# The order of the first six attention units in an attention and experts kernel on one Trainium2 core

## The chip, the core and the metric

The kernel runs on one core of a Trainium2 chip. It uses TensorE (PE: matmuls, with weight loads shown apart as PEld), VectorE (DVE), ScalarE (ACT), GpSimd (POOL) and the DMA queues that SyncE (SP), ACT and POOL fill. The metric is the device time of one execution in microseconds; lower is better. A profile is one execution, taken by the hardware profiler.

## The reference

Block-sparse attention (4 batches, 8 heads, 768 tokens, head size 64, blocks of 32), then a mixture of 4 experts in which every token uses every expert.

```python
mask = np.abs(blk_i - blk_j) <= 1                      # own block and its two neighbours
mask |= (blk_i == 0) | (blk_j == 0) | (blk_i == n_blocks - 1) | (blk_j == n_blocks - 1)
for qb in range(n_blocks):
    for kb in sampled_blocks[qb]:                      # three sampled blocks for each block
        mask[qb * 32:(qb + 1) * 32, kb * 32:(kb + 1) * 32] = True
scores = np.where(mask, q @ k.T / 8, -1e9)
attn = softmax(scores) ; x = attn @ v                  # x: 3072 tokens x 512
for e in range(4):
    h = np.maximum(x @ w1[e], 0.0)                     # 512 -> 1024
    out += p[:, e:e+1] * (h @ w2[e])                   # 1024 -> 512
```

## The kernel before, in words

An inner block of 32 queries sees eight blocks of keys: three neighbours, the two end blocks and three sampled ones. Four such blocks make a group `t` of 128 queries, and a group is done in two **units** (`u` = 0 and 1, four heads each). Before the experts can start, three groups of batch 0 must be done: units 0 to 5, groups 0 to 2. This document calls that stretch the **opening**. After it the expert products keep PE busy, with the other attention units put between them.

A unit n (class `Group`) goes through these steps. `S(n)`: scores on PE (L304 against the neighbours in `k`, L309 against the gathered keys `kr`), 64 matmuls, then on DVE four maxima with the mask (L319) and on ACT four exponentials (L322). `T(n)`: eight transposes of the probabilities on PE (L331) in two halves, the first copied to `pt` by ACT and the second by DVE (L333). `A(n)`: 64 matmuls with the values (L359), then on DVE the reciprocal sums `rec` (L348, L349) and the weighting into `xg` (L377). `X(n)`, for odd n: four transposes of the group's result (L403), then `tokens` casts it to the experts' operand `xo` on ACT (L281) and puts the rest on DVE (L282).

What the units need: keys `kr` of a group are copied inside SBUF by POOL, ACT and DVE (L149 end blocks, L156 sampled blocks, whose number is read into a register first, L141). Values `v` of a group are two tiles: neighbours by SP (L175) and sampled rows by four gathers that POOL issues (L179, `DMA_INDIRECT`); the end blocks' values lie in `ends` and are copied in (`put_ends`, L852). There are four value tiles, so group 2 reuses those of group 0 when `A(1)` has read them. The mask is made from index tables on POOL and DVE and spread to rows by one matmul (L256).

The experts' weights come as `w1` (`load_w1`, L580, 512 KB; two halves s = 0, 1 for each of eight chunks c) and `w2` (`load_w2`, L585, 256 KB). A half of `w1` becomes four operands `wo`: ACT casts (L597), POOL makes the rest (L598). A `w2` tile becomes `h` (ACT, L635) and `l` (POOL, L636) in `split_w2`. Seven `wo` are made before the first product; each product then asks for the next. A `w1` load must wait until POOL is done with the fourth `wo` of the half that lies in its buffer, a `w2` load until POOL has made `l` of the tile in its buffer. A first-layer product pair (L662, two `wo`) writes the accumulators `v` and `w` in turn; ACT takes the result by a ReLU (`hh`, L671) and DVE the rest (`hl`, L672), and only then is the accumulator free again. Second-layer matmuls are L732.

All five engines run their instructions in the order in which the program writes them; SP issues its loads in that order too, and one that must wait holds those behind it.

Of the kernel before, what the change touches and what calls it, by code (L numbers as in the profile page):

```python
# [17 lines left out]
P = 128  # L18
BLOCK = 32
# [4 lines left out]
def attention_moe_kernel(ctx: ExitStack, tc, qb, kb, vr, sampled, sampled_t, probs, w1, w2, out):  # L24
# [37 lines left out]
    pool["k"] = setup.enter_context(tc.tile_pool(name="k1", bufs=8))  # L62
# [73 lines left out]
    def copier(j, r):  # L136
        return nc.scalar if j <= QG and r == 2 else COPIERS[r % len(COPIERS)]

    def sampled_block(j, r):
        if (j, r) not in regs:  # L140
            regs[j, r] = copier(j, r).value_load(sbrow[:1, j * NR + r, :1], min_val=0, max_val=NB - 1)  # L141
        return regs[j, r]
# [15 lines left out]

    def end_rows(b):
        return bass.AP(vr.tensor, vr[b * S:b * S + BLOCK].offset,  # L160
                       [[DM, BLOCK], [(NB - 1) * BLOCK * DM, 2], [1, DM]])
# [7 lines left out]
    def load_v(b, t, cs=range(QG)):  # L169
        js = blocks(t)  # L170
        for c in range(min(cs), min(max(cs) + 1, len(js)), 2):
# [3 lines left out]
            nc.sync.dma_start(v[:3 * BLOCK, :n, 0],  # L175
                              bass.AP(rows.tensor, rows.offset,
                                      [[DM, 3 * BLOCK], [BLOCK * DM, n], [1, DM]]))
            for i in range(n):
# [11 lines left out]
    for c in range(QG):  # L190
        for r in (1, 2):
            sampled_block(1 + c, r)
# [28 lines left out]
                   allow_small_or_imprecise_dtypes=True)  # L221
    bad = p1.tile([NB, SLOTS], F32, name="bad")
    sbf = p1.tile([NB, NR], F32, name="sbf")
    d = p1.tile([NB, NR], F32, name="d")
    nc.gpsimd.memset(bad, 0.0)
    nc.vector.tensor_copy(sbf, sbi[:, :, 0])
# [7 lines left out]
    for r in range(1, NR):  # L234
        for e in range(r):
# [3 lines left out]
    ind = p1.tile([NB, NG, P], F32, name="ind")  # L239
    nc.gpsimd.memset(ind, 1.0)  # L240
    nc.gpsimd.affine_select(out=ind, in_=ind, pattern=[[P, NG], [1, P]], compare_op=ALU.is_ge,
                            fill=0.0, base=BLOCK, channel_multiplier=-BLOCK)
    nc.gpsimd.affine_select(out=ind, in_=ind, pattern=[[-P, NG], [-1, P]], compare_op=ALU.is_ge,
                            fill=0.0, base=-1, channel_multiplier=BLOCK)
    ind4 = p1.tile([NB, P], F32, name="ind4")
    nc.vector.reduce_sum(ind4, ind.rearrange("n t p -> n p t"), axis=AX.X)
    sel = p1.tile([NB, NG, SLOTS], F32, name="sel")
    nc.gpsimd.memset(sel, -BIG)
    nc.gpsimd.affine_select(out=sel, in_=sel, pattern=[[-QG, NG], [0, SLOTS]], compare_op=ALU.is_ge,
# [781 lines left out]
```

## Time and profile before

| | us |
|---|---|
| time, median of 3 runs (lowest to highest) | 1254.86 (1254.47 to 1259.41) |
| the profiled execution: its own time | 1257.47 |
| the profiled execution: span of its instructions | 1255.6 |
| first expert product starts (in the span) | 49.17 |
| PE busy in the span | 1231.8 (98%) |

Times in rows count from the start of the span. In a row of a timeline stand the start, the length, the engine, the line, the operation, what it writes and reads with sizes, how many instructions were merged, and in brackets how long the engine stood idle before and what ended that. "issue" means that the engine waited for nothing that the profile shows.

### The profile page before, as it was taken

How to read it: one execution, taken by the hardware profiler on the slowest of the kernel's cores; microseconds unless marked ns; L12 is line 12 of the kernel's file. 1: busy time of each engine (PE TensorE's matmuls, PEld its weight loads, DVE VectorE, ACT ScalarE, POOL GpSimd, SP SyncE). 2: the span in 40 equal slices, each digit the busy share in tenths (PEclk: the TensorE clock that was granted, in tenths of full speed). 3: DMA queues.
4: the chain of work that ended last, by engine and by line, in shares of the span. 5: the costliest groups of instructions: out<-in, count | busy, mean ns of one | idle time of the engine just before them, and what ended most of it. 6: DMA issues, size and time to landing. Idle time of an engine off the chain costs nothing.

```text
span 1255.6 us, 31597 instructions
## 1 busy us (share of the span) xinstructions
PE 1231.8 (98%) x12242; PEld 1072.5 (85%) x12242; DVE 753.9 (60%) x1735; ACT 679.5 (54%) x1826; POOL 719.0 (57%) x848
## 2 busy tenths in 40 slices
PE   6899999999999999999999999999999999999998
PEld 4788888888888888888888888888888899999997
DVE  6455535555458675666658676665756855555553
ACT  5556645666655546666555455666664544444441
POOL 6566556666659545555547655556544855555550
PEclk9899999999999999999999999999999999999999
DMA  9546555655535325332323433333321222222211
GB/s 258 181 128 170 153 183 170 192 174 173 159 111 188 110 68 156 98 118 90 111 86 120 145 102 100 103 119 114 118 77 43 93 93 67 68 68 68 67 51 51
DMA packets 64113, 149.02 MB, mean 119 GB/s; under 512 B 7707, under 2 KB 9244, under 8 KB 63964
## 3 DMA queue, kind: packets, MB, share of 16 engines
q1 hardware_dynamic: 58294, 129.70, 32.9%
q0 software_dynamic: 5632, 17.31, 5.1%
q8 instruction: 96, 1.57, 0.5%
q14 instruction: 53, 0.43, 0.1%
q10 hardware_dynamic: 38, 0.00, 0.0%
HBM read 140.69 MB, written 6.29 MB: 117 GB/s over the span
## 4 chain that ended last, share of the span: by engine, by line
PE 67%; DVE 1%; issue 1%; POOL 0%; POOLq 0%; DVEq 0%
PE po L732 33%; PE w L683 16%; PE v L683 12%; PE o L359 2%; PE tp L331 1%; PE s L309 1%; PE s L304 1%; DVE oacc L747 1%; PE ow L469 1%; PE sw L418 1%; PE tw L440 0%; DVE r L619 0%; POOL wo L612 0%; DVE r L617 0%; PE v L662 0%
## 5 line engine op out<-in xcount | busy, mean ns | idle before, releaser
L612 POOL TENSOR_TENSOR wo<-r,wo 128x256 fp32r<-128x256 f32 x288 | 241.1, 840 | 279.7 <-ACT wo L611 278.1
L732 PE MATMUL po<-h,hh 128*128 128x512 f32 x768 | 310.2, 404 | 1.3 <-DVE oacc L747 1.1
L732 PE MATMUL po<-h,hl 128*128 128x512 f32 x768 | 302.6, 394 | 0.0
L732 PE MATMUL po<-l,hh 128*128 128x512 f32 x768 | 301.7, 393 | 0.0
L683 PE MATMUL w<-xo,wo 128*128 128x384 f32 x1152 | 236.1, 340 | 0.0
L636 POOL TENSOR_TENSOR l<-r,h 128x512 fp32r<-128x512 f32 x160 | 211.4, 1321 | 37.5 <-ACT h L635 37.0
L683 PEld LDWEIGHTS w<-xo,wo 128*128 128x128 f32 x1152 | 207.5, 188 | 18.0 <-DVE z L718 0.7
L683 PE MATMUL v<-xo,wo 128*128 128x384 f32 x864 | 175.9, 338 | 0.0
L732 PEld LDWEIGHTS po<-h,hl 128*128 128x128 f32 x768 | 144.2, 188 | 33.0
L683 PEld LDWEIGHTS v<-xo,wo 128*128 128x128 f32 x864 | 154.4, 188 | 12.3 <-ACT z L710 0.2
L732 PEld LDWEIGHTS po<-h,hh 128*128 128x128 f32 x768 | 144.2, 188 | 19.6 <-DVE oacc L747 2.9
L598 POOL TENSOR_TENSOR wo<-r,wo 128x256 fp32r<-128x256 f32 x128 | 95.3, 747 | 114.7 <-ACT wo L597 109.3
L732 PEld LDWEIGHTS po<-l,hh 128*128 128x128 f32 x768 | 145.2, 189 | 11.4
L611 ACT CAST wo<-r 128x256 fp32r<-128x256 f32 x288 | 114.5, 398 | 49.7 <-PE w L683 32.2
L747 DVE SCALAR_TENSOR_TENSOR oacc<-po,pr,oacc 128x512 f32<-128x512 f32 x168 | 124.3, 742 | 24.6 <-PE po L732 24.4
L322 ACT ACTIVATE p<-p,mx 128x256 f32<-128x256 f32 (+1 forms) x192 | 95.5, 499 | 69.4 <-DVE mx L319 67.5
L635 ACT CAST h<-r 128x512 fp32r<-128x512 f32 x160 | 99.3, 620 | 11.8 <-PE po L732 11.8
L179 POOL DMA_INDIRECT v<-in_vr_dram,vidx x88 | 85.7, 974 | 26.3 <-issue 16.6
L319 DVE CUSTOM_DVE_ANT_1 p<-s,mask 128x256 f32<-128x256 f32 (+1 forms) x192 | 69.9, 418 | 46.3 <-PE s L309 45.9
L662 PE MATMUL v<-xo,wo 128*128 128x384 f32 x384 | 79.9, 345 | 0.5 <-ACT xo L281 0.5
L706 DVE TENSOR_TENSOR p<-w,p 128x384 f32<-128x384 f32 x48 | 26.7, 556 | 89.4 <-PE w L683 82.3
L662 PE MATMUL w<-xo,wo 128*128 128x384 f32 x384 | 79.1, 341 | 0.0
(139 smaller groups left out, 1723.4 us busy)
## 6 DMA issues: line engine op xcount, KB each, us to landing
r<-in_w_dram SPq DMA_DIRECT2D x80, 512.0 KB, 4.0
r<-in_w_dram SPq DMA_DIRECT2D x160, 256.0 KB, 2.7
v<-in_vr_dram SPq DMA_DIRECT2D x44, 384.0 KB, 4.8
k<-in_kb_dram SPq DMA_DIRECT2D x8, 768.0 KB, 5.7
v<-in_vr_dram SPq DMA_DIRECT2D x12, 512.0 KB, 5.1
out_dram<-oacc SPq DMA_DIRECT2D x23, 256.0 KB, 2.5
q<-in_qb_dram SPq DMA_DIRECT2D x20, 256.0 KB, 5.2
v<-in_vr_dram SPq DMA_DIRECT2D x24, 128.0 KB, 3.4
```

The source lines that it names most:

```text
L179: nc.gpsimd.indirect_dma_start(out=v[:G, i, 1], out_offset=None, in_=vr, element_offset=b * S * DM, in_offset=bass.IndirectOffsetOnAxis(ap ...
L319: nc.vector.tensor_tensor_reduce(p.rearrange("p (a b) -> p a b", b=BLOCK), s[h][:n, i], mk, -SCALE, 3.0e38, ALU.add, ALU.min, mx[:n])
L322: nc.scalar.activation(p, p, AF.Exp, bias=mx[:n], scale=-1.0, accum_out=self.sums[:n, m:m + 1])
L598: nc.gpsimd.tensor_sub(o[:, 1], r[s][:, i, k], f32(o[:, 0]))
L611: nc.scalar.copy(o[:, 0], src)
L612: nc.gpsimd.tensor_sub(o[:, 1], src, f32(o[:, 0]))
L635: nc.scalar.copy(h, r)
L636: nc.gpsimd.tensor_sub(l, r, f32(h))
L662: nc.tensor.matmul(W[s], w[:, wi, t], x[xi][:, k * KH + t], start=k == 0 and m == 0, stop=k == 1 and m == 3 * KH - 1)
L683: nc.tensor.matmul(ps, w[:, wi, t], x[:, xi, t], start=fresh and m == 0, stop=m == 3 * KH - 1, skip_group_check=not fresh)
L732: nc.tensor.matmul(p, a[:, js], w, start=f == 0 and n == 0, stop=f == FT - 1 and n == 2)
L747: nc.vector.scalar_tensor_tensor(accs[tok], p, pe, accs[tok], op0=ALU.mult, op1=ALU.add)
```

## The change

Only the opening is written anew. Its parts:

- **Engines' orders.** Scores and softmax of a unit are split (`S`, `soft`), so that the ACT copy of the previous unit's transposes stands between the second and third exponential. `X(1)` and `X(3)` move behind `A(2)` and `A(4)`, and `A(4)` moves ahead of `T(5)`.
- **Keys.** A group has one tile instead of four, and its end blocks are copied by one DVE instruction (`group_keys`). Sampled blocks go to other engines (`copier`): in group 0 POOL copies 4, ACT 6, DVE 2; in groups 1 and 2 POOL and ACT 6 each. Registers for group 0 (ACT: groups 0 and 1) are read ahead of the copies. Group 2's copies on ACT come as three after unit 2's exponentials and three after unit 3's.
- **End values.** `put_ends` copies half of the columns at a time, all on DVE.
- **Mask.** Two small matmuls (`sps`, `mps`) with small index tables replace one with a 24x768 table (`ind`).
- **Loads.** The second half of chunk 0's `w1`, three `w2` tiles and `qe` are issued behind group 2's values.
- **Weights.** `wo` and `split_w2` come later: two `wo` each after units 4 and 5, and three of the four `split_w2` after the last token cast.

```diff
     def copier(j, r):
-        return nc.scalar if j <= QG and r == 2 else COPIERS[r % len(COPIERS)]
+        if first_units[0]:
+            if j <= QG:
+                return (nc.gpsimd, nc.scalar, nc.vector if j % 2 else nc.scalar)[r]
+            return nc.gpsimd if (j + r) % 2 else nc.scalar
+        return COPIERS[r % len(COPIERS)]
...
+    def group_keys(t):
+        ks = kept.get(t % 2) or pool["k"].tile([P, QG, NR + 2, P], F32, name="kr")
+        if t < 2:
+            kept[t] = ks
+            nc.vector.tensor_copy(ks[:, :, 0:NR + 2:NR + 1],
+                                  keys[0][0][:, 0:NB:NB - 1].unsqueeze(1).broadcast_to([P, QG, 2, P]))
+        gathered[0, t][1].update((c, ks[:, c]) for c in range(QG))
...
-    ind = p1.tile([NB, NG, P], F32, name="ind")
...
+    nc.tensor.matmul(sps.rearrange("p t n -> p (t n)"), turns, sel.rearrange("p t n -> p (t n)"),
+                     start=True, stop=True)
...
+        def put_ends(n, u):
+            e = slice(u * 2 * HH * D, (u + 1) * 2 * HH * D)
+            nc.vector.tensor_copy(kept["v"][n][3 * BLOCK:, :, :, e],
+                                  kept["ends"][3 * BLOCK:, :, e].unsqueeze(1)
+                                  .broadcast_to([BLOCK, 2, 2, 2 * HH * D]))
...
+        for n in range(NG + 2):
+            if n < NG:
+                us[n].S()
             if n >= 2:
                 us[n - 2].A()
+            if 4 <= n < NG + 1 and n % 2 == 0:
+                us[n - 3].X()
+            if 1 <= n <= NG:
+                copies[n - 1] = [us[n - 1].T(i) for i in range(2)]
+            if n < NG:
+                us[n].soft(copies[n - 1][0] if n else None)
+            elif n == NG:
+                copies[n - 1][0]()
+            if n in (2, 3, 4):
+                for i in range(2):
+                    put_ends(*((i, 1), (2 + i, 0), (2 + i, 1))[n - 2])
+            if n >= 2:
+                us[n - 2].G()
+            if 1 <= n <= NG:
+                copies[n - 1][1]()
...
             if n == 1:
                 load_q(0, 2)
-                copy_k(0, 2)
-                for s in range(2):
-                    load_w1(0, s)
+                group_keys(2)
+                load_w1(0, 0)
+                copy_some(2, nc.gpsimd)
+            if n in (2, 3):
+                copy_some(2, nc.scalar, slice(3 * (n - 2), 3 * (n - 1)))
+            if n == 3:
+                load_v(0, 2)
+                load_edge_q(0)
+                load_w1(0, 1)
                 for f in range(3):
                     load_w2(f)
...
+        us[NG - 1].X()
+        us[NG - 1].C([slice(0, KH), slice(KH, HP)])
+        next(weights)
+        split_w2(1)
+        for f in range(2, 4):
+            split_w2(f)
```

`copy_some` issues the sampled-block copies of one engine, `G` holds the reciprocal and weighting that `A` held, `C` the token casts that `X` held.

**PE, the last units.** First the kernel before: `S(5)` (four rows), `A(3)`, `T(4)`, `X(3)`, `T(5)`, then `A(4)` and `A(5)` in one row, `X(5)`.

```order
L304 MATMUL s<-k,q 32x96 x8
L309 MATMUL s<-kr,q 32x160 x8
L304 MATMUL s<-k,q 32x96 x8
L309 MATMUL s<-kr,q 32x160 x8
L359 MATMUL o<-v,pt 32x64 x32
L331 MATMUL tp<-ident,p 128x128 x8
L403 MATMUL x<-ident,xg 128x128 x4
L331 MATMUL tp<-ident,p 128x128 x8
L359 MATMUL o<-v,pt 32x64 x64
L403 MATMUL x<-ident,xg 128x128 x4
```

The same place of the changed kernel, from `S(5)`'s last row: `A(3)`, `T(4)`, `A(4)`, `X(3)`, `T(5)`, `A(5)`, `X(5)`.

```order
L345 MATMUL s<-kr,q 32x160 x8
L406 MATMUL o<-v,pt 32x64 x32
L375 MATMUL tp<-ident,p 128x128 x8
L406 MATMUL o<-v,pt 32x64 x32
L453 MATMUL x<-ident,xg 128x128 x4
L375 MATMUL tp<-ident,p 128x128 x8
L406 MATMUL o<-v,pt 32x64 x32
L453 MATMUL x<-ident,xg 128x128 x4
```

`A(4)` now follows `T(4)` at once and stands ahead of `X(3)` and `T(5)`; `A(5)` follows `T(5)` at once.

**POOL, the weights around the end of the opening.** Before, from group 2's four gathers on; the tile behind `wo<-` is the half of `w1` that it is made from: r_685 and r_687 are chunk 0, r_1123 is chunk 1.

```order
L179 DMA v<-in_vr_dram,vidx 96x512 x4
L598 TENSOR_TENSOR wo<-r_685,wo 128x256 x2
L636 TENSOR_TENSOR l_1017<-r_689,h_1016 128x512
L598 TENSOR_TENSOR wo<-r_685,wo 128x256
L636 TENSOR_TENSOR l_1126<-r_691,h_1125 128x512
L598 TENSOR_TENSOR wo<-r_687,wo 128x256 x2
L636 TENSOR_TENSOR l_1233<-r_693,h_1232 128x512
L598 TENSOR_TENSOR wo<-r_687,wo 128x256
L636 TENSOR_TENSOR l_1242<-r_1020,h_1241 128x512
L598 TENSOR_TENSOR wo<-r_687,wo 128x256
L598 TENSOR_TENSOR wo<-r_1123,wo 128x256 x4
```

The same stretch of the changed kernel; r_560 and r_890 are chunk 0.

```order
L207 DMA v<-in_vr_dram,vidx 96x512 x4
L650 TENSOR_TENSOR wo<-r_560,wo 128x256 x4
L650 TENSOR_TENSOR wo<-r_890,wo 128x256
L688 TENSOR_TENSOR l_1182<-r_892,h_1181 128x512
L650 TENSOR_TENSOR wo<-r_890,wo 128x256 x2
L688 TENSOR_TENSOR l_1240<-r_894,h_1239 128x512
L688 TENSOR_TENSOR l_1246<-r_896,h_1245 128x512
L688 TENSOR_TENSOR l_1252<-r_1185,h_1251 128x512
L650 TENSOR_TENSOR wo<-r_890,wo 128x256
```

Three `l` in a row now stand ahead of the eighth `wo`, the last of r_890, and all of them behind the seventh `wo`, whose cast follows the last token cast on ACT.

**SP, the loads of the opening.** Before, from group 2's `q` on: both halves of `w1`, three `w2`, `qe`, then group 2's values.

```order
L130 DMA q<-in_qb_dram 128x512
L580 DMA r_685<-in_w_dram 128x1024
L580 DMA r_687<-in_w_dram 128x1024
L585 DMA r_689<-in_w_dram 128x512
L585 DMA r_691<-in_w_dram 128x512
L585 DMA r_693<-in_w_dram 128x512
L110 DMA qe<-in_qb_dram 128x2x128
L175 DMA v<-in_vr_dram 96x2x512 x2
```

The same place of the changed kernel:

```order
L130 DMA q<-in_qb_dram 128x512
L632 DMA r_560<-in_w_dram 128x1024
L203 DMA v<-in_vr_dram 96x2x512 x2
L110 DMA qe<-in_qb_dram 128x2x128
L632 DMA r_890<-in_w_dram 128x1024
L637 DMA r_892<-in_w_dram 128x512
L637 DMA r_894<-in_w_dram 128x512
L637 DMA r_896<-in_w_dram 128x512
```

Group 2's values moved ahead of `qe`, of the second half of `w1` and of the three `w2`; the number of loads is the same.

## Rows read from the trace of the kernel before

**Rows 1.** The page: busy time of each engine with its share of the span and its instructions; and from its list of groups the exponentials: count, busy time, mean ns of one, idle time ahead and what ended most of it.
```profile
PE 1231.8 (98%) x12242; PEld 1072.5 (85%) x12242; DVE 753.9 (60%) x1735; ACT 679.5 (54%) x1826; POOL 719.0 (57%) x848
...
L322 ACT ACTIVATE p<-p,mx 128x256 f32<-128x256 f32 (+1 forms) x192 | 95.5, 499 | 69.4 <-DVE mx L319 67.5
```

**Rows 2.** Busy time by stretches: stretch, length, busy time of PE, PEld, DVE, ACT and POOL (instructions), granted PE clock as a share of full speed, busy share of the DMA engines, GB/s.
```profile
40.00:45.00 5.00, 5.00 (x125) 4.51 (x120) 2.90 (x8) 4.53 (x14) 2.14 (x3) 0.77 0.17 52
...
49.10:1255.60 1206.50, 1200.19 (x11408) 1048.73 (x11408) 722.79 (x1624) 651.42 (x1740) 688.14 (x795) 1.00 0.37 115
```

**Rows 3.** Timeline of PE in the opening.
```profile
11.40 0.72 PE L309 MATMUL s<-kr,q 64*32 64x160 f32 x4 [0.51 <-POOL kr L156]
...
20.57 0.43 PE L359 MATMUL o<-v,pt 128*32 128x64 f32 x14 [1.48 <-ACT pt L333]
21.46 1.41 PE L359 MATMUL o<-v,pt 128*32 128x64 f32 x50 [0.46 <-DMA v<-in_vr_dram,vidx]
...
27.71 1.09 PE L359 MATMUL o<-v,pt 128*32 128x64 f32 x62 [1.32 <-issue]
28.73 1.09 PE L331 MATMUL tp<-ident,p 128*128 128x128 f32 x8
...
31.71 0.47 PE L309 MATMUL s<-kr,q 64*32 64x160 f32 x6 [0.75 <-issue]
...
38.27 0.27 PE L304 MATMUL s<-k,q 64*32 64x96 f32 x2 [2.68 <-issue]
...
40.68 1.86 PE L331 MATMUL tp<-ident,p 128*128 128x128 f32 x8
...
43.91 1.99 PE L359 MATMUL o<-v,pt 128*32 128x64 f32 x128
...
48.27 0.44 PE L403 MATMUL x<-ident,xg 128*128 128x128 f32 x2 [1.47 <-DVE xg L377]
49.17 3.89 PE L662 MATMUL v<-xo,wo 128*128 128x384 f32 x12 [0.46 <-ACT xo L281]
52.90 2.24 PE L662 MATMUL w<-xo,wo 128*128 128x384 f32 x12
```

**Rows 4.** Timeline of POOL in the opening: the table `ind`, key copies, gathers, `l`.
```profile
2.79 0.86 POOL L241 TENSOR_SCALAR_AFFINE_SELECT ind<-ind 24x768 f32<-24x768 f32 x1
...
8.99 0.40 POOL L156 COPY kr<-k 128x128 f32 x1 [1.15 <-DMA k<-in_kb_dram]
...
10.43 1.15 POOL L156 COPY kr<-k 128x128 f32 x2 [0.34 <-issue]
...
13.54 0.92 POOL L179 DMA_INDIRECT v<-in_vr_dram,vidx  x1 [0.31 <-issue]
...
19.86 2.00 POOL L179 DMA_INDIRECT v<-in_vr_dram,vidx  x1 [0.30 <-issue]
...
46.18 1.27 POOL L636 TENSOR_TENSOR l<-r,h 128x512 fp32r<-128x512 f32 x1
...
52.03 0.73 POOL L598 TENSOR_TENSOR wo<-r,wo 128x256 fp32r<-128x256 f32 x1 [2.68 <-ACT wo L597]
```

**Rows 5.** Timeline of DVE in the opening: end keys, end values, and the reciprocal sums of units 4 and 5.
```profile
8.95 0.99 DVE L149 COPY kr<-k 128x256 f32<-128x256 f32 x4 [0.26 <-DMA k<-in_kb_dram]
9.97 1.22 DVE L852 COPY v<-ends 32x2048 f32<-32x2048 f32 x1
...
19.38 2.36 DVE L852 COPY v<-ends 32x2048 f32<-32x2048 f32 x2
...
40.26 0.17 DVE L348 TENSOR_SCALAR rec<-sums 128x4 f32<-128x4 f32 x1
...
45.03 0.53 DVE L348 TENSOR_SCALAR rec<-sums 128x4 f32<-128x4 f32 x1
...
46.22 1.25 DVE L348 TENSOR_SCALAR rec<-sums 128x4 f32<-128x4 f32 x1
```

**Rows 6.** Timeline of ACT: a key copy, the copy of `T(5)`'s first half, the last token cast, the first casts from chunk 1's second half of `w1`.
```profile
16.42 0.30 ACT L156 COPY kr<-k 128x128 f32 x1 [0.42 <-issue]
...
43.68 0.60 ACT L333 COPY pt<-tp 128x512 f32<-128x512 f32 x1
...
49.60 0.37 ACT L281 CAST xo<-x 128x256 fp32r<-128x256 f32 x1 [0.49 <-DVE xo L282]
...
58.66 0.71 ACT L597 CAST wo<-r 128x256 fp32r<-128x256 f32 x2 [0.91 <-DMA r<-in_w_dram]
```

**Rows 7.** Timeline of all engines around the fourth, fifth and sixth product pair.
```profile
59.34 0.49 ACT L671 ACTIVATE hh<-w 128x384 fp32r<-128x384 f32 x1
...
59.86 0.56 DVE L672 SCALAR_TENSOR_TENSOR hl<-w,hh 128x384 fp32r<-128x384 f32 x1 [1.52 <-ACT hh L671]
...
61.91 1.22 PE L662 MATMUL w<-xo,wo 128*128 128x384 f32 x6
```

**Rows 8.** Timeline of SP: issues of loads.
```profile
15.40 0.92 SPq L580 DMA_DIRECT2D r<-in_w_dram  x2
...
52.78 0.33 SPq L580 DMA_DIRECT2D r<-in_w_dram  x1
```

**Rows 9.** DMA by queue in the stretch 35.5 to 37 us: packets, MB, share of 16 engines.
```profile
q8 instruction: 1, 0.02, 5.1%
```

**Rows 10.** The line L580 (loads of `w1`, the whole run): from issue to landing.
```profile
DMA to landing us min/median/max: 3.2/4.0/11.7
```

More of the change, by code (lines that the diff above doesn't have):

```diff
@@ L157, in copy_k, with copy_some @@
                 gathered[b, t][1][c] = k
+    def group_keys(t):
[5 more added lines that the diff above has]
+        gathered[0, t][1].update((c, ks[:, c]) for c in range(QG))
+    def copy_some(t, eng, some=slice(None)):
+        copy = eng.copy if eng is nc.scalar else eng.tensor_copy
+        for c, j, r in [(c, j, r) for c, j in enumerate(blocks(t)) for r in range(NR)
+                        if copier(j, r) is eng][some]:
+            copy(gathered[0, t][1][c][:, 1 + r:2 + r], keys[0][0][:, bass.ds(sampled_block(j, r), 1)])
     def end_rows(b):
@@ L167, in with_ends, with load_v @@
         return v
-    def load_v(b, t, cs=range(QG)):
+    def load_v(b, t, cs=range(QG), parts=(True, True)):
         js = blocks(t)
@@ L323, in S @@
                                          accum_out=self.sums[:n, m:m + 1])
+                if i == 0 and between:
+                    between()
         def T(self, i):
@@ new lines, in attention_moe_kernel @@
+        read_blocks(0, nc.gpsimd)
+        load_v(0, 0, (0, 1))
+        load_v(0, 0, (2, 3), (True, False))
+        kept["vi"] -= 1
+        read_blocks(0, nc.vector)
+        load_q(0, 1)
+        for t in range(2):
+            group_keys(t)
+            if t == 0:
+                for eng in COPIERS:
+                    copy_some(0, eng)
+                make_identity(nc, ident)
+                load_v(0, 0, (2, 3), (False, True))
+        copy_some(1, nc.scalar)
+        copy_some(1, nc.gpsimd)
@@ L879, in attention_moe_kernel @@
                 for f in range(3):
                     load_w2(f)
-                load_edge_q(0)
-            if n == 3:
-                load_v(0, 2)
-            if n >= 2:
+            if n in (4, 5):
                 next(weights)
-            if n >= 4:
-                split_w2(n - 4)
-        us[NG - 3].X()
-        us[NG - 1].T(0)
-        us[NG - 1].T(1)
-        us[NG - 2].A()
-        us[NG - 1].A()
-        for n in range(3):
-            next(weights)
-            if n:
-                split_w2(n + 1)
@@ L897, in attention_moe_kernel @@
-        us[NG - 1].X(1)
+                next(weights)
+            if n == NG:
+                next(weights)
+                split_w2(0)
+                next(weights)
+        us[NG - 1].X()
+        us[NG - 1].C([slice(0, KH), slice(KH, HP)])
+        next(weights)
+        split_w2(1)
+        for f in range(2, 4):
+            split_w2(f)
         pool["p"] = pp
```

132 lines of the change are left out of this document (72 added, 60 removed).

## The prediction

> **What bounds the kernel now.** I read the busy times first: PE is busy for 98% of the span [rows 1]. Then I cut the span where the first expert product starts, at 49.17 [rows 3]. From there to the end PE is busy for 1200.19 of 1206.50 us, at full clock [rows 2]. The change leaves PE's order after this point as it is, so nearly all that it can give is an earlier start of that first product, and nearly all that it can lose afterwards is a new wait of the product stream. The opening is 3.9% of the span: 0.5% of the time (6.3 us, about what a measurement of this kernel can tell from no change) would be an eighth of it.
>
> So the timeline of PE in the opening comes next. The reader should look at what stands in brackets. `S(0)` gets its last keys at 11.40, behind a POOL copy. `A(0)` begins at 20.57, when the copy of `T(0)` is there, and goes on at 21.46, when the last gather of group 0 has landed [rows 3]. After that, up to the end of `T(4)` at 42.54 (40.68 + 1.86), PE waits for no engine at all: its idle pieces of 1.32, 0.75 and 2.68 us are all "issue" [rows 3]. The third of them falls together with an instruction load: 16 KB on queue q8 in the stretch from 35.5 to 37 [rows 9]. Behind it the granted clock is 0.77 of full in 40 to 45, which mixes the two levels of 2.4 and 1.2 GHz [rows 2], and `T(4)` takes 1.86 us where `T(2)` took 1.09 [rows 3]. The tail, from 42.54 to 49.17, is a chain: `A(4)` with `A(5)` to 45.90, the weightings on DVE, `X(5)` at 48.27, the token cast, the product.
>
> **The mask and group 0's keys: nothing by themselves.** The table `ind` goes (one select on it is 0.86 us of POOL [rows 4]), key copies run without register loads between them (0.34 and 0.42 us of "issue" before one [rows 4, 6]), end keys take one DVE instruction instead of four. All this ends before `A(0)`, which waits for the gather until 21.46 whatever `S(0)` to `T(0)` do; that wait is the cover. Without the cover these edits would be worth the 0.89 us between the two starts of `A(0)`, and more ahead of it. What counts is when the fourth gather of group 0 is issued and lands.
>
> **The gather in front of `A(0)`: -1.0 us (from -2.0 to +0.8).** POOL issues it at 13.54, and PE goes on 7.9 us later [rows 3, 4]. Ahead of it stand four key copies from 8.99 to 11.58. Without register loads four of 0.3 us would end near 10.2, which is -1.4. The `w1` and `w2` loads that SP issued from 15.40 on [rows 8] while the gather was under way shrink from 1.8 MB to 0.5 MB; for the quieter queues I allow another -0.6, an estimate: 7.3 us to PE instead of 7.9. Against this stands DVE. POOL's pair of copies at 10.43 took 1.15 us while DVE copied end values from 9.97 to 11.19, and the gather issued at 19.86 took 2.00 instead of 0.92 while DVE did the same from 19.38 to 21.74 [rows 4, 5]. The change puts more of this on DVE just here: end keys of two groups (0.99 us each at the old price), two sampled copies, two half end values (0.61 each). If POOL is held throughout, its fourth copy ends near 12.4, +0.8. I take the middle, nearer to the gain, because in the old trace copies did come through between DVE's short ones (0.40 us at 8.99).
>
> The Trainium skill, page "SBUF — State Buffer", section "Who interferes with whom", has a rule on this that speaks against the change: a VectorE copy in a two-port mode holds the port pair that GpSimd needs for its whole length, and GpSimd fully blocks, descriptors of its DMAs included. By that rule the trace agrees (2.00 beside 0.92 us), and the sum would take +0.8 here, 1.8 more than mine.
>
> **From `A(0)` to `T(4)`: +0.4 us (from 0 to +1.0), and the stalls unsettled by 1.4 either way.** PE runs the same instructions; only `X(1)` moves behind `A(2)`. A PE that waited for no engine here cannot be fed faster. One wait is new: group 2's last three key copies on ACT stand behind unit 3's exponentials, and those behind the copy of `T(2)`. From `T(2)`'s middle that is 0.6 for the copy, 1.0 for two exponentials (0.5 each [rows 1]) and, at 0.7 a copy with register load, 2.1 less what is read ahead while ACT works, some 2.5 to 3.0 in all. `S(4)` needed the keys 3.0 us after `T(2)` began and then had its 0.75 of "issue" [rows 3], so I add 0.4. The copies of group 2 on POOL stand ahead of nothing but its gathers, which must wait for `A(1)` anyway. Group 2's values, issued at the end of `A(1)` as before but now ahead of the weights, have the 16 us to `A(4)` that they had (27.71 to 43.91). The three "issue" gaps stay where they are; the third may shrink to the 1.32 of the first (-1.4) or a fourth of that size may come in `A(4)`, because the `w1` and `w2` loads moved behind group 2's values now fill the queues after `A(1)`, where the old trace grows quiet (DMA 0.17 in 40 to 45 [rows 2]).
>
> **The tail: -0.5 us (from -1.3 to +0.6).** Before, 6.63 us from the end of `T(4)` to the product. In the new order `A(4)` follows `T(4)` at once and must wait for DVE's copy of its second half, 0.6 to 0.7; it ends 1.3 after `T(4)`, `X(3)` at 1.9, `T(5)` at 3.0, `A(5)` (again behind a DVE copy) at 4.2, unit 5's weighting at 4.7, `X(5)` at 5.3, and the product at 5.8 (-0.85). Before, DVE's `rec` took 0.53 and 1.25 us for units 4 and 5 instead of 0.17, beside POOL's `l` from 46.18 [rows 4, 5]; in the new order a `wo`, an `l` and a `wo` run on POOL just when unit 5 is weighted, so one such loss of up to 1.1 can stay. In between lies -0.5.
>
> **The later batches: nothing.** There 12 key copies go from ACT to DVE and some registers are read again; 12 times 0.25 us [rows 5] on a DVE that is busy for 723 of 1206 us [rows 2].
>
> **The product stream after the start: +0.8 us (from 0 to +2.0).** This is the place that I expect readers to miss. Call the new start T'. Three `split_w2` now follow the last token cast. That cast ends 0.80 after the product starts (49.60 + 0.37 against 49.17 [rows 3, 6]); then the seventh `wo` (cast 0.4, POOL 0.73), three `l` of 1.27 and the eighth `wo` of 0.73 end at T' + 6.5, where the eighth ended at T + 3.6 before (52.03 + 0.73) [rows 4]. SP issues the second half of chunk 1's `w1` only then (52.78 before [rows 8]), and behind a `w2`, the probabilities and a value load that wait for the third `l`: T' + 7.1, which is 3.5 later. Behind this load wait two casts (0.71) on ACT, behind them the fourth pair's `hh`, then `hl` on DVE, and then the accumulator that the sixth pair writes. Before, from issue to cast was 5.88 us, ACT already idled 0.91, and `hl` ended at 60.42, 1.49 ahead of the sixth pair [rows 6, 7]. Now the cast starts at T' + 11.1 (with the median landing of 4.0 [rows 10]) or T' + 13.0 (with 5.88), `hl` ends 1.76 later, and the sixth pair is due at T' + 12.74. That is a wait of 0.1 to 2.0. A first pair at full clock (2.24 instead of 3.89 us [rows 3]) would not help: what it gives is lost again here, as long as the load sets the sixth pair.
>
> **The sum.** -1.0 + 0.4 - 0.5 + 0.8 = -0.3 us. On the profiled execution (1257.47, of which 1.87 outside the span) that is 1257.2; that execution was 2.6 above the median, so against the median of 1254.86 I predict 1254.6.
>
> **Rivals.**
> - *PE is freed* (faster). If DMA is quieter, the instruction load does not stall `S(5)`, the low clock behind it goes with it (`T(4)` lost 0.77 us to it [rows 3], `A(3)` ahead of it about as much: -1.6), and the gather comes early: -2.0 - 1.4 - 1.6 - 0.5 + 0.8 = -4.7, 1250.2. For it speaks that the old opening loses 4.75 us to such gaps; against it, that the new one issues the same bytes. Past 0.5% it comes only if the first pair runs at full clock too (-1.65) and the sixth doesn't wait (-0.8): 1247.8.
> - *The late `w1` load decides* (slower). If it lands more than 3.9 us after T' + 7.1, each further microsecond is lost. With 8 us it is 4.1, with the 11.7 that the longest of these loads took [rows 10] 7.8. With the other terms at their sum of -1.1: 1257.9 and 1261.6. For it speaks that ACT already waited on this load; against it, that the old slack of 1.49 was enough.
> - *DVE's copies hold POOL* (the change does not do what it says). Gathers are issued no earlier, `A(0)` comes 0.8 later, the tail keeps its `rec`: +0.8 + 0.4 + 0.6 + 0.8 = +2.6, 1257.5.
>
> **How the numbers follow.** The forecast, no change to speak of, has 0.50; PE freed 0.20; the late load 0.17; POOL held 0.13. Of PE freed, 0.08 lies past 0.5%; of the late load, 0.05 lies past it on the other side. So faster 0.08, same 0.87, slower 0.05. The range goes from 1250.0, where the first rival's milder sum ends, to 1259.0, a microsecond above the second's; all four terms and the stalls at their ends at once would give 1250.2 (-3.3 - 1.4) and 1260.7 (+4.4 + 1.4), and the upper of these needs mishaps in every place. The likeliest case by itself runs from 1252 to 1257.
>
> **What would show it right or wrong.** Right: the first gather-bound `A(0)` near 20.5, "issue" gaps of PE still there, a bracket that names a POOL or ACT key copy in `S(4)`, `A(4)` waiting for `pt`, the first product between 46 and 49, and an ACT idle before the cast of chunk 1's second half longer than 0.91. Wrong: a first product ahead of 44, or a sixth pair that follows the fifth without a wait, or a second low stretch of clock in the products. The sum fails most easily at the gather and at the landing of that `w1` load, since both depend on queues that the old trace shows under another load.

## The result, and the profile after

| | before | changed |
|---|---|---|
| time, median of 6 runs each (lowest to highest), us | 1256.91 (1254.47 to 1259.41) | 1263.87 (1261.62 to 1265.10) |
| ratio to before, with its 95% interval | 1 | 1.0056 (1.0044 to 1.0067) |
| the profiled execution: span, us | 1255.6 | 1263.4 |
| first expert product starts | 49.17 | 50.67 |
| sixth product pair starts | 61.91 | 69.68 |
| from there to the end | 1193.69 | 1193.72 |

The changed kernel is 7 us slower, and the forecast of no change to speak of, 1254.6 (1250.0 to 1259.0), is wrong: 1263.87 is 4.9 above its upper end, on the side to which it gave 0.05. The last three lines of the table place the loss in this pair of traces, whose spans are 7.8 apart. The opening ends 1.50 us later than in the trace of before; between the first and the sixth product pair another 6.27 us go; from the sixth pair on the two traces take the same time to 0.03 us. A second pair of traces (after_again and before_again, below) has +0.08, +7.40 and -1.88 in the same three places. So the product stream is the one place that loses in both, and the opening and the later batches show no cost beyond what single executions differ by.

Timeline of PE in the changed kernel (columns as in [rows 3]); the rows answer to those of `A(0)`, `S(4)`, `S(5)`, `T(4)` and the product pairs there and in [rows 7].

```profile
17.95 0.35 PE L406 MATMUL o<-v,pt 128*32 128x64 f32 x9
...
22.15 0.97 PE L406 MATMUL o<-v,pt 128*32 128x64 f32 x50 [2.68 <-DMA v<-in_vr_dram,vidx]
...
28.89 0.53 PE L345 MATMUL s<-kr,q 64*32 64x160 f32 x8
30.33 0.46 PE L345 MATMUL s<-kr,q 64*32 64x160 f32 x4 [0.91 <-ACT kr L184]
...
39.97 0.28 PE L340 MATMUL s<-k,q 64*32 64x96 f32 x4 [4.83 <-issue]
...
42.46 1.75 PE L375 MATMUL tp<-ident,p 128*128 128x128 f32 x8
...
50.67 2.46 PE L714 MATMUL v<-xo,wo 128*128 128x384 f32 x12 [0.46 <-ACT xo L317]
52.98 2.24 PE L714 MATMUL w<-xo,wo 128*128 128x384 f32 x12
61.21 3.77 PE L714 MATMUL v<-xo,wo 128*128 128x384 f32 x12 [5.99 <-DVE hl L724]
64.82 2.24 PE L714 MATMUL w<-xo,wo 128*128 128x384 f32 x12
...
69.68 1.22 PE L714 MATMUL w<-xo,wo 128*128 128x384 f32 x6
```

The bracket to look at is the third pair's: PE stands 5.99 us because the accumulator of the first pair is not free, and that is free only when DVE has made `hl`. So the question is why DVE is late. Its timeline, and those of SP and POOL in the same stretch (SP's rows are issues of loads; a row's length there holds the waits between its issues):

```profile
59.59 0.25 DVE L879 TENSOR_REDUCE psum_e<-pr 128x24 f32<-128x96 f32 x1 [7.65 <-DMA pr<-in_probs_dram]
...
60.61 0.55 DVE L724 SCALAR_TENSOR_TENSOR hl<-v,hh 128x384 fp32r<-128x384 f32 x1
...
50.20 6.49 SPq L637 DMA_DIRECT2D r<-in_w_dram  x4
56.74 0.43 SPq L878 DMA_DIRECT2D pr<-in_probs_dram  x1
...
57.96 0.46 SPq L632 DMA_DIRECT2D r<-in_w_dram  x1
...
52.57 3.77 POOL L688 TENSOR_TENSOR l<-r,h 128x512 fp32r<-128x512 f32 x3
```

Read from the bottom up: POOL makes the three `l` in a row until 56.34. SP's last of four `w2` loads needs the third of them, so SP is held until then. Behind it on SP stands the load of the experts' probabilities `pr`, issued at 56.74. On DVE four small instructions that normalise these probabilities (L879 to L882) stand ahead of `hl` of the first pair, and the first waits 7.65 us for the load. `hh` had been there since 54.05 (53.56 + 0.49).

The kernel before has the same chain, with a little room in it. Timeline of DVE and SP before, the rows of that load and of who waits for it:

```profile
52.05 0.25 DVE L827 TENSOR_REDUCE psum_e<-pr 128x24 f32<-128x96 f32 x1 [1.62 <-DMA pr<-in_probs_dram]
...
49.76 0.42 SPq L826 DMA_DIRECT2D pr<-in_probs_dram  x1
```

DVE waited for the load there too, 1.62 us, and `hl` still followed `hh` by a third of a microsecond. It ended at 54.31, 0.67 us ahead of the third pair; in before_again, where the first pair ran at full clock, the third pair waited 0.24 us for it. The change issues the load 6.98 us later, and 1.50 of that is the later start of the products.

The pause costs more than itself. Busy times by stretches (columns as in [rows 2]) around it:

```profile
50.00:55.00 5.00, 4.54 (x26) 4.07 (x24) 0.85 (x2) 3.94 (x10) 3.99 (x5) 1.00 0.19 56
55.00:60.00 5.00, 0.22 (x2) 0.00 (x0) 0.37 (x2) 0.79 (x2) 4.06 (x6) 0.75 0.75 226
60.00:65.00 5.00, 3.79 (x14) 3.79 (x14) 1.55 (x5) 0.41 (x1) 0.74 (x1) 0.57 0.72 256
```

The granted clock is full while the first two pairs run, falls to the half level (1.2 GHz) while PE stands, and stays there when PE starts again (0.50 of full from 57.5 to 64.3): the third pair takes 3.77 instead of 2.24 us. Together: 5.99 + 1.53, less 1.42 because the first pair now runs at full clock (2.31 us to the second instead of 3.73 [rows 3]), is 6.10 of the 6.27 us. The 1.42 belong to that one execution of the kernel before: in before_again its first pair runs at full clock too (2.30 us to the second).

### The profile page after: what moved, and what is told of

It is laid out like the page before. It is cut to its first block, busy times and chain, and to the rows that moved or that the text cites. A ratio compares the mean times of both kernels' runs of the same rounds, so it can differ in the third digit from the quotient of the medians.

```text
span 1263.4 us, 31667 instructions
## 1 busy us (share of the span) xinstructions
PE 1231.6 (97%) x12244; PEld 1071.5 (85%) x12244; DVE 761.1 (60%) x1741; ACT 675.0 (53%) x1815; POOL 718.9 (57%) x854
## 4 chain that ended last, share of the span: by engine, by line
PE 67%; DVE 1%; issue 1%; POOL 0%; POOLq 0%; DVEq 0%
PE po L784 32%; PE w L735 16%; PE v L735 12%; PE o L406 2%; PE tp L375 1%; PE s L345 1%; PE s L340 1%; DVE oacc L799 1%; PE ow L521 1%; PE sw L470 1%; PE tw L492 0%; DVE r L671 0%; POOL wo L664 0%; DVE r L669 0%; PE v L714 0%
## 5 line engine op out<-in xcount | busy, mean ns | idle before, releaser
L735 PEld LDWEIGHTS v<-xo,wo 128*128 128x128 f32 x864 | 154.4, 188 | 12.3 <-ACT z L762 0.2
L714 PEld LDWEIGHTS v<-xo,wo 128*128 128x128 f32 x384 | 69.6, 192 | 12.5 <-DVE hl L724 6.3
```

Of the source, the lines that this page charges most:

```text
L714: nc.tensor.matmul(W[s], w[:, wi, t], x[xi][:, k * KH + t], start=k == 0 and m == 0, stop=k == 1 and m == 3 * KH - 1)
L735: nc.tensor.matmul(ps, w[:, wi, t], x[:, xi, t], start=fresh and m == 0, stop=m == 3 * KH - 1, skip_group_check=not fresh)
```

## The experiments

Each kernel was timed beside the kernel before on the same chip. The four rows marked "slower chip" come from one on which the kernel before took 1272.85 us, 1.3% more than elsewhere, so ratios are compared, not times. The table has each kernel's ratio and, from its trace, where `A(0)` goes on for its main part (behind the last gather, or in before_again and before_splits behind ACT's copy), the idle piece in `S(5)`, the first product, and the waits of the third and the sixth pair for `hl`.

| kernel | ratio (95%) | A(0) | S(5) piece | first product | 3rd pair | 6th pair |
|---|---|---|---|---|---|---|
| before | 1 | 21.46 | 2.68 | 49.17 | 0 | 0 |
| before_again | one run | 20.26 | 0.78 | 48.07 | 0.24 | 0 |
| changed | 1.0056 (1.0044 to 1.0067) | 22.15 | 4.83 | 50.67 | 5.99 | 0 |
| after_again | 1.0042 (1.0030 to 1.0054) | 20.34 | 3.97 | 48.15 | 6.30 | 0 |
| before_splits | 1.0047 (1.0031 to 1.0063) | 20.92 | 0.81 | 47.56 | 6.49 | 0 |
| pr_early | 1.0017 (1.0008 to 1.0027) | 20.68 | 3.98 | 48.24 | 0 | 3.67 |
| pr_loads | 1.0015 (1.0003 to 1.0028) | 20.03 | 0.62 | 45.33 | 0 | 2.13 |
| ends_act | one run | 19.87 | 3.69 | 45.77 | 6.10 | 0 |
| pr_splits | 0.9992 (0.9980 to 1.0004) | 20.51 | 4.01 | 47.22 | 0 | 1.24 |
| all_three_again | 0.9970 (0.9960 to 0.9979) | 20.81 | 1.83 | 45.88 | 0 | 0 |
| splits_only (slower chip) | 1.0006 (0.9996 to 1.0017) | | | 52.36 | 3.17 | 0 |
| pr_loads_splits (slower chip) | 0.9992 (0.9982 to 1.0003) | | | 52.88 | 0 | 0.81 |
| all_three (slower chip) | 0.9983 (0.9973 to 0.9993) | | | 53.79 | 0 | 0 |
| before_pr (slower chip) | 1.0014 (1.0004 to 1.0025) | | | 56.11 | 0 | 0 |

**pr_early: the load alone.**

```diff
                 for f in range(3):
                     load_w2(f)
+                nc.sync.dma_start(pr, probs)
...
     def token_weights():
-        nc.sync.dma_start(pr, probs)
         nc.vector.reduce_sum(psum_e, pr, axis=AX.X)
```

> The changed kernel with one load moved: SP issues the probabilities' load behind the third w2 of the opening instead of behind the seventh. DVE's four instructions on them stay where they are. Theory A (the probabilities held the stream): the load lands long before DVE asks for it, hl of the first pair follows hh at once, the third product pair follows the second without a wait (5.99 us gone), and as PE does not pause, its clock does not fall and the third pair takes 2.24 instead of 3.77 us: 7.5 us less, about 1256.4 at the median. Rival B (the prediction's own reason: the late second half of chunk 1's w1): that load is still issued near 57.6, when the third l of the three in a row is done, and its casts come near 62 to 63.6; hl of the fourth pair then ends near 64 to 65, and the sixth pair, due near 62, waits 2 to 3.5 us, so that only 2.5 to 5.5 us come back: 1258.5 to 1261.5.

Of the waits both theories were right, one behind the other. Timelines of PE, SP and ACT:

```profile
52.63 2.27 PE L714 MATMUL v<-xo,wo 128*128 128x384 f32 x12
...
63.43 2.29 PE L714 MATMUL w<-xo,wo 128*128 128x384 f32 x6 [3.67 <-DVE hl L724]
...
55.10 0.46 SPq L632 DMA_DIRECT2D r<-in_w_dram  x1
...
61.68 0.71 ACT L649 CAST wo<-r 128x256 fp32r<-128x256 f32 x2 [6.26 <-DMA r<-in_w_dram]
```

The third pair follows without a wait and at full clock. But the second half of chunk 1's `w1` is issued at 55.10, is there 6.58 us later, and ACT stands 6.26 us for it; so the sixth pair waits 3.67, and its first six matmuls take 2.29 us instead of 1.22, again behind a pause (the granted clock is 0.50 of full from 63.4 to 66.6). This is the wait that the prediction described; in the changed kernel it lies under the longer one. The ratio falls from 1.0056 to 1.0017, about 5 us (3 us against the 1.0042 of after_again): inside rival B's 2.5 to 5.5 either way, and at least 2.5 short of theory A's 7.5.

**before_splits: one part of the change in the kernel before.** Three of the four `split_w2` and the seventh `wo` move behind the last token cast, and the first `split_w2` goes between the fifth and the sixth `wo`, as in the changed kernel; nothing else moves.

```diff
-            if n >= 4:
-                split_w2(n - 4)
...
-        for n in range(3):
-            next(weights)
-            if n:
-                split_w2(n + 1)
+        next(weights)
+        split_w2(0)
+        next(weights)
         us[NG - 1].X(1)
+        next(weights)
+        for f in range(1, 4):
+            split_w2(f)
```

> The kernel before with one part of the change alone: three of the four split_w2, and the seventh wo, come behind the last token cast; everything else is as before. Theory A: POOL ends the third l of the three near 54.8 instead of 49.35, SP can issue the fourth of the following w2 loads only then and the probabilities' load behind it near 55.2 (before 49.76), it lands near 58, hl of the first pair ends near 59, and the third pair, due near 55.3, waits 3.5 to 4.5 us; the clock falls behind the pause (up to 1.5 us more): 4 to 6 us slower than before, 1261 to 1263. Rival C (the place of the splits is harmless, and the loss comes from the new orders of keys and loads in the opening): within 1 us of before.

Timelines of PE, SP and DVE:

```profile
58.59 4.21 PE L662 MATMUL v<-xo,wo 128*128 128x384 f32 x12 [6.49 <-DVE hl L672]
...
53.62 0.42 SPq L826 DMA_DIRECT2D pr<-in_probs_dram  x1
...
56.97 0.25 DVE L827 TENSOR_REDUCE psum_e<-pr 128x24 f32<-128x96 f32 x1 [8.15 <-DMA pr<-in_probs_dram]
```

This part alone reproduces the loss: 1.0047, 5.9 us, beside 1.0056 and 1.0042 of the changed kernel, with the same chain on the same three engines. The wait is 2 us above what was expected: the first pair ran at full clock here, so the third was due 1.4 earlier, and the load took 3.35 from issue to DVE instead of 2.8. Rival C (the loss comes from the orders of keys and loads) falls.

**splits_only and before_pr: the two other corners.** In splits_only the four `split_w2` of the changed kernel stand where the kernel before has them (after units 4 and 5 and among the last `wo` of the opening; only the fourth stays behind the last cast):

```diff
             if n in (4, 5):
                 next(weights)
                 next(weights)
+                split_w2(n - 4)
             if n == NG:
                 next(weights)
-                split_w2(0)
+                split_w2(2)
                 next(weights)
...
-        split_w2(1)
-        for f in range(2, 4):
-            split_w2(f)
+        split_w2(3)
```

> The changed kernel with the four split_w2 back at the places of the kernel before (after units 4 and 5 and around the last two wo of the opening; only the fourth stays behind the last token cast); the probabilities' load stays at its place behind the w2 loads. Theory A (that load waits for the last l on POOL): the l of the fourth split now ends 2.5 to 3 us earlier against the first product, so the third pair waits 2.5 to 3.5 instead of 5.99 us: about 3 us less than the changed kernel, near 1260. Rival H (the splits' place is all that matters): the wait goes, and 6 to 7.5 us with it.

before_pr is the kernel before with the load of pr_early:

```diff
                 load_edge_q(0)
+                nc.sync.dma_start(pr, probs)
             if n == 3:
```

> The kernel before with the probabilities' load alone moved ahead of group 2's values. There DVE waited 1.62 us for it and hl still followed hh by 0.33 us, with the third pair not waiting, so theory A expects no change: within 0.3% of before. If the load's place mattered already before the change, it would gain 0.5 us and more.

In splits_only the third pair waits 3.17 us, as theory A had it; the load is issued at 55.95, 3.59 after the first product, where the changed kernel has 6.07. The ratio, 1.0006, is lower than the 1.003 of theory A's 1260, and why was not followed; as the changed kernel itself did not run on that chip, the ratio decides nothing against rival H. The wait does: by rival H it would be gone. before_pr gains nothing: where the load was in time, its place does not matter (the 0.14% above 1 is unexplained; none of its second to sixth product pairs waits for another engine).

**pr_loads: the order of the loads.** To pr_early's edit comes:

```diff
-                load_w1(0, 0)
+                for s in range(2):
+                    load_w1(0, s)
+                for f in range(3):
+                    load_w2(f)
+                load_edge_q(0)
+                nc.sync.dma_start(pr, probs)
                 copy_some(2, nc.gpsimd)
...
                 load_v(0, 2)
-                load_edge_q(0)
-                load_w1(0, 1)
-                for f in range(3):
-                    load_w2(f)
```

> The kernel of the first run, and besides the second half of chunk 0's w1, the three w2, qe and the probabilities are issued where the kernel before issued them, ahead of group 2's values. Theory D (the 4.83 us in S(5) are an instruction load that stands behind the 2 MB issued from 27.67 on): the queues are quiet from about 36 on, the load of 16 KB comes near 35.5 as before, the idle piece in S(5) falls to 2.0 to 2.7 us, and the time is 2 us below that of the first run, unless A(0) pays for it: its last gather then shares the queues with 1.3 MB more (0 to 1 us). Rival E (the piece is set by when PE asks for its next block of instructions): it stays between 4.3 and 4.9, and the time within 0.7 us of the first run.

Theory D holds for the place, not for the time. DMA by queue in the changed kernel, 36.5 to 38.5 us, in which the instruction load falls (columns as in [rows 9]):

```profile
q1 hardware_dynamic: 149, 0.27, 50.5%
q0 software_dynamic: 96, 0.27, 49.7%
q8 instruction: 1, 0.02, 4.0%
```

The 16 DMA engines are full with values and weights (the three shares), and the instruction load starts at 37.26, 2.12 us after PE ran dry (34.80 + 0.34); in before it started at 35.58, when PE had just stopped. Over all traces the piece in `S(5)` is 3.69 to 4.83 where the weights are issued behind group 2's values (five traces) and 0.62 to 2.68 where they are issued ahead of them (five traces on the same kind of chip). On the slower chip it is 1.36 in splits_only, with the weights behind, and there is none in the three kernels with the weights ahead. But look at the timeline of PE in pr_loads:

```profile
25.48 1.66 PE L406 MATMUL o<-v,pt 128*32 128x64 f32 x64 [2.33 <-ACT p L364]
...
35.60 0.28 PE L340 MATMUL s<-k,q 64*32 64x96 f32 x4 [0.62 <-issue]
```

The piece of 2.33 ahead of `A(1)` is put down to ACT, but an instruction load ends 1.40 ahead of its end, at 24.08; in the changed kernel that load lay under `A(0)`'s wait. So a part of the stall moved forward. In these two traces the first product still comes 2.91 us earlier than in pr_early, but 1.6 of that are lost again before the third pair, as the first two pairs of pr_loads ran in part at the half level (3.61 and 2.73 us). The ratios of pr_early and pr_loads (1.0017 and 1.0015) can't be told apart, so no gain of time from the order of the loads is shown.

**ends_act: who holds POOL.** The two first copies of end values go to ACT (`put_ends(n, 0, nc.scalar.copy)`).

> The changed kernel with the two first copies of end values on ACT instead of DVE (11.19 to 12.57). Theory F (DVE's copies hold POOL): the two instructions that make the identity on POOL take 0.20 and 0.29 again instead of 0.76 and 0.62, the fourth gather of group 0 is issued near 13.2 to 13.4 instead of 14.17, and A(0) goes on near 21.3 instead of 22.15. Rival G (the gathers land when the queues are through with the values and weights ahead of them): an earlier issue does not land earlier, and A(0) goes on at 21.9 to 22.3. The stream behind is as in the changed kernel: a wait of about 6 us at the third pair.

Timelines of POOL, first the changed kernel and then ends_act: the two instructions that make the identity, and the fourth gather of group 0.

```profile
11.27 0.76 POOL masks.py:197 MEMSET ident<- 128x128 f32 x1
12.10 0.62 POOL masks.py:199 TENSOR_SCALAR_AFFINE_SELECT ident<-ident 128x128 f32<-128x128 f32 x1
...
14.17 0.92 POOL L207 DMA_INDIRECT v<-in_vr_dram,vidx  x1 [0.31 <-issue]
```

```profile
11.34 0.19 POOL masks.py:197 MEMSET ident<- 128x128 f32 x1
11.60 0.29 POOL masks.py:199 TENSOR_SCALAR_AFFINE_SELECT ident<-ident 128x128 f32<-128x128 f32 x1
...
13.34 0.92 POOL L207 DMA_INDIRECT v<-in_vr_dram,vidx  x1 [0.31 <-issue]
```

Theory F holds for POOL: beside DVE's two copies (11.19 to 12.57 in the changed kernel) the two instructions took 1.38 us (0.89 in after_again), without them 0.48, and the gather is issued 0.83 earlier. The Trainium skill, page "SBUF — State Buffer", section "Who interferes with whom", has this as a lock of the shared ports; the traces agree, with these numbers. That the earlier issue brings `A(0)` forward is not shown. `A(0)` goes on at 19.87, earlier than theory F (21.3) and rival G (21.9 to 22.3) had it. From that issue to `A(0)` it is 7.98 us in the changed kernel, 6.53 here, and 6.75 and 6.36 in after_again and pr_early, whose program is that of the changed kernel up to then. And in all_three_again, where the gather is issued at 13.25, `A(0)` goes on at 20.81, no earlier than in those two.

**after_again and before_again: the spread of one execution.**

> The changed kernel once more, for a second trace of its opening. What comes from the program should stand again: third pair waiting 5.5 to 6.5 us for hl, an idle piece of 3.5 to 5 us in S(5), some 0.5% slower than before. What belongs to the single execution may move: the start of A(0) behind its last gather (22.15) by up to 1.5 us, and with it the first product (50.67).

> The kernel before once more, for a second trace of its opening: no wait at the third pair; idle pieces of PE in the opening between 0.5 and 2.7 us each; first product between 47.5 and 50.5 if the spread of the single execution is 1.5 us.

The wait of the third pair (6.30) and the piece in `S(5)` (3.97) stand again, the ratio is 1.0042. Timelines of PE, first before_again and then after_again, the third and the sixth pair:

```profile
52.85 2.35 PE L662 MATMUL v<-xo,wo 128*128 128x384 f32 x12 [0.24 <-DVE hl L672]
...
59.90 1.22 PE L662 MATMUL w<-xo,wo 128*128 128x384 f32 x6
```

```profile
59.02 3.64 PE L714 MATMUL v<-xo,wo 128*128 128x384 f32 x12 [6.30 <-DVE hl L724]
...
67.38 1.22 PE L714 MATMUL w<-xo,wo 128*128 128x384 f32 x6
```

From the first to the sixth pair that is 11.83 and 19.23 us, 7.40 more: 6.06 by the wait and 1.29 by the third pair's lower clock. The first product, 1.50 us later in the first pair of traces, now comes at 48.15 against 48.07. So neither a gain nor a loss of the opening as a whole is shown. `A(0)` moved by 1.81 us and the first product by 2.52 between the two traces of the changed kernel, more than the 1.5 allowed for: the terms of a single trace in the opening are good to some 1.5 to 2.5 us.

**pr_splits, pr_loads_splits, all_three: what is left when the waits go.** pr_splits is pr_early with the edit of splits_only; pr_loads_splits is pr_loads with it; all_three is pr_loads_splits with the edit of ends_act, and ran twice.

> The changed kernel with the probabilities loaded early and the split_w2 at the places of the kernel before; the weights are still issued behind group 2's values. Theory A with B': no wait of the third pair, at most 1 us at the sixth; theory D: the idle piece in S(5) is still 3.5 to 5 us. The time then is that of the kernel before within 0.3%: what the opening gains elsewhere (1 to 2 us) the piece in S(5) takes. Rival J (the order of the loads does not matter for the time): equal to the next kernel of this list within 0.1%.

> The third run (probabilities loaded early, weights ahead of group 2's values) with the four split_w2 at the places of the kernel before. Theory B' (two waits stood one behind the other: the probabilities, and behind them the second half of chunk 1's w1, which SP may issue only when POOL is through with the l in front of the eighth wo): the eighth wo is made some 2.5 us earlier against the first product, the w1 load is issued as much earlier, and the wait of the sixth pair (2.13 in the third run) goes or stays under 0.5: 2 us below the third run, about the time of the kernel before or up to 2 us under it. Rival I (the load's landing of 6 us and more in the crowded queues decides): the wait stays between 1.5 and 2.5.

> The kernel ahead of this in the list, and the first two copies of end values on ACT as in the fourth run. Fourth gather of group 0 issued near 13.3, A(0) goes on near 20, first product between 44.5 and 46.5 (49.17 in the kernel before), no wait above 1 us in the product stream: 1251 to 1254 if the earlier first product is kept to the end. If the opening's gain is a matter of the single execution, it comes out with the kernel before, 1254 to 1257.

> The kernel with all three repairs once more, since the chip of its first runs was slower for every kernel: no product wait above 1 us and a ratio to the kernel before between 0.996 and 0.999.

pr_splits came out as the kernel before (0.9992), with 1.24 at the sixth pair, a little above the 1 expected, and 4.01 in `S(5)`. all_three_again, with the loads and the end copies moved too, is at 0.9970 on the same chip, so the equality that rival J forecast is not there; but which of the two edits gives how much of these 2.8 us was not separated, and that the order of the loads alone is worth time stays unshown (pr_early beside pr_loads says nothing for it). Theory B' shows in both kernels with the splits put back: the late `w1` half is issued 4.33 and 4.40 us behind the first product (pr_splits, pr_loads_splits) instead of 6.86 and 6.91 (pr_early, pr_loads), and the sixth pair's wait falls from 3.67 to 1.24 and from 2.13 to 0.81, the latter 0.3 above the 0.5 that was expected. The 2.13 of pr_loads is the smaller one only because its slow first pairs made the sixth due 1.55 us later. all_three is faster than the kernel before on both chips, 0.9983 and 0.9970; the second is 3.8 us by the ratio (3.1 between the medians). Timeline of PE in all_three_again, and its stretches from 15 us on:

```profile
45.88 2.47 PE L714 MATMUL v<-xo,wo 128*128 128x384 f32 x12 [0.46 <-ACT xo L317]
...
50.27 2.24 PE L714 MATMUL v<-xo,wo 128*128 128x384 f32 x12
...
57.25 1.32 PE L714 MATMUL w<-xo,wo 128*128 128x384 f32 x6
```

```profile
15.00:45.80 30.80, 21.35 (x700) 16.46 (x698) 21.13 (x72) 20.48 (x68) 17.36 (x26) 1.00 0.72 210
45.80:1251.20 1205.40, 1199.17 (x11408) 1046.64 (x11408) 729.50 (x1636) 649.09 (x1730) 688.57 (x797) 1.00 0.37 115
```

The first product is at 45.88, no pair waits, and the granted clock is at the full level in both stretches. With these three repairs the changed kernel is 2 to 4 us ahead of the kernel before.

## Why the prediction was wrong, point by point

- **The mask and group 0's keys, nothing:** right. `A(0)` begins at 17.95, 2.62 earlier than before, and then waits for the gather, as before.
- **The gather, -1.0 (-2.0 to +0.8):** +0.69 in the first pair of traces, +0.08 in the second, and the sign of the issue was wrong: 14.17 (13.57 to 14.34 in the seven traces whose program is the same up to there) where before had 13.54 and 13.24. The copies without register loads did not save 1.4 us: four of them took 1.79 beside DVE's end keys. And the register loads had not gone but stand ahead of the first gather, which is issued at 7.19 instead of 5.52 (that order put back was not tried). The third rival had the later issue right.
- **`A(0)` to `T(4)`, +0.4 and the stalls unsettled by 1.4:** +0.98 (22.06 us from where `A(0)` goes on to the end of `T(4)`, 21.08 before). `S(4)` waits 0.91 and 0.19 for ACT's key copies, where 0.4 were allowed. The copies came about when they were forecast, but the row of `S(4)` was misread: the 3.0 us after `T(2)` began are where its last six matmuls start, behind the idle 0.75 and not ahead of it, and in the changed kernel `S(4)` stops for these keys already 1.74 after (28.89 + 0.53 - 27.68). The pieces of 1.32 and 0.75 went, and the third grew from 2.68 to 4.83. That more loads in the queues could lengthen a stall was thought of for `A(4)`, not for the instruction load in `S(5)`.
- **The tail, -0.5:** -0.17 (6.46 instead of 6.63 from the end of `T(4)`). DVE's `rec` of unit 5 took 0.50 us (1.25 before [rows 5]), and `X(5)` and the casts followed as forecast. In range.
- **Later batches, nothing:** no cost shows. The agreement to 0.03 us is luck; in the second pair of traces the same stretch differs by 1.88 us the other way.
- **The product stream, +0.8 (0 to +2.0):** this is the step that failed; it measured +6.27, and +7.40 in the second pair of traces. Its working was right as far as it went: the eighth `wo` ended at T' + 6.3 (6.5 forecast; the first of the row at 56.29), SP issued the late `w1` half at T' + 7.29 (7.1 forecast), and alone, in pr_early, it makes the sixth pair wait 3.67 (0.1 to 2.0 forecast, as the load takes 6.58 and not 4.0 to 5.88 us, and the first pair runs at full clock). But the sentence that put the probabilities behind the third `l` on SP went on to the load behind them, and did not ask who waits for the probabilities, so their wait stood at nothing. It measured 5.99 us (6.30 and 6.10 in after_again and ends_act). Who waits is DVE, ahead of `hl` of the first pair, which the third pair needs 4.55 us after the first starts (52.98 + 2.24 - 50.67), long before the sixth is due. The clock's fall behind the pause was not in the sum either, though a second low stretch of clock in the products stood among the signs of being wrong, and came.
- **The rivals:** "the late `w1` load decides" was the nearest, right in kind and in the engines that hold the load, wrong in which load comes first. That its price of up to 7.8 at the longest landing is near the loss is luck: the loss came by another chain, and this load took 6.58 us and not 11.7. PE freed showed in part, later, as all_three.

What is shown: the moved splits are enough for the loss (before_splits), and the probabilities' load is what carries it to the third pair (pr_early). What stays open: how all_three's gain divides over the gather, the instruction loads and the tail, and why splits_only costs less time than its wait.

## What to carry to other kernels

When work is moved later on one engine, write down every load that its buffers hold back on an in-order queue, and for each of them the first instruction that asks for it and what stands behind that instruction; a load of 48 KB with an unrelated purpose can be the one that decides. Removing the first wait of such a chain shows the next one (6 us became 3.7), so look for the second before taking the first as the price. And a pause of the bottleneck engine in the middle of dense work can be paid twice, once as the pause and once at the half clock behind it. Here that was so behind each of the waits of 3.17 us and more, and not behind the 2.13 us of pr_loads, where the clock stayed full. Last, a term that one pair of traces gives to 0.03 us may still be 2 us off in the next pair.

## What the runs showed of the hardware that was not expected

An instruction load of 16 KB on queue q8 shares the DMA engines with the data. In the changed kernel, with all of them busy, it started 2.12 us after PE had run dry, and the idle piece in `S(5)` was 4.83 us; in the four other traces with the weights behind group 2's values (same kind of chip) it started 1.27 to 1.43 us after. In the five traces with the weights ahead of them it started up to 1.90 us before PE ran dry. In these ten traces and in splits_only PE went on 1.24 to 1.46 us after the load's end (38.53 to 39.97 in the changed kernel), so the end of the load fits as what PE waits for where the profile says "issue".

Chips differ. On the slower one the opening of before_pr shows ten pieces of "issue", 6.6 us in all, where before had five with 5.2 us (2.7 in 1, 1.3 in 1, 1.2 in 3). Waits of PE in before_pr (total us, times, longest); a tenth piece, of 0.97, stands ahead of `A(1)`:

```profile
PE s L304 <- issue: 3.7, 7, 1.2
PE s L309 <- issue: 1.9, 2, 0.9
```

Its first product came at 56.11 instead of 48 to 49 us. The pieces explain little of that, and the keys landed 1.8 us later there (POOL's first copy at 10.77 instead of 8.99); the rest was not followed.

The granted clock was at the half level when PE started again behind each of the five long waits of the third pair (3.17 to 6.49 us; the pair then took 3.64 to 4.21 instead of 2.24) and behind the sixth pair's 3.67 in pr_early. It stayed full behind the sixth pair's 2.13, 1.24 and 0.81 (pr_loads, pr_splits, pr_loads_splits; six matmuls in 1.31 us), and through all products of all_three_again. A waiting pair is not the only thing ahead of a fall: the first pairs of before (3.89 us) and pr_loads (3.61 us) ran wholly or in part at the half level behind the idle pieces of the tail, and in all_three, on the slower chip, four short pieces in one attention unit between the products (142.9 to 145.1) were followed by 0.50 of full from 146.6 to 149.9.
